# A seven-product mm2: ScalarE copies the first product's PSUM bank in two halves, each behind its row block, with mm1's last activation behind both

## The chip, the cores and the metric

The kernel runs on one core of a Trainium2 chip. The metric is device time in microseconds (us) of one execution. TensorE is called PE, and its weight loads PEld; VectorE is DVE, ScalarE is ACT, GpSimd is POOL, SyncE is SP. Each engine works off its own queue in order, and engines wait for one another through semaphores. Matrix products are accumulated in PSUM, which has eight banks of 128 partitions x 512 f32; the other memory is SBUF.

## The reference: chunk attention, then a two-layer MLP

```python
# q, k, v: 8 batches, 8 heads, 576 rows, 64 columns, f32; chunks of 64 rows
scores = scale * q_chunk @ k_chunk.T            # 64 x 64 within a chunk
attn = softmax(scores)
x = (attn @ v_chunk) -> [4608 tokens, 512]      # the heads side by side
h = gelu_exact(x @ w_in)                        # 512 -> 2048
out = h @ w_out                                 # 2048 -> 512
```

Attention is small. Most of the work is the two matrix products of the MLP: mm1, with the gelu behind it, and mm2.

## The kernel before

**Tiles.** The tokens are cut into nine tiles of 512. Tiles 0 to 7 hold the first eight chunks of one batch each; tile 8 holds the ninth chunks of all eight batches. The loop over t (at the end of the kernel) runs `phase(t, ...)`, which is mm1 and then mm2 of tile t. The attention of tile t + 1 is put into mm2 of tile t by small functions in the dictionary `e2`: the functions under key i are run where mm2 says `also(i)`. Weights and activations are bf16, sums are f32. The order of every engine's work is the order in which the program issues it; no scheduler changes it. The tile framework adds the semaphore waits, by the tiles that instructions read and write.

**Seven products.** From tile 3 on (`FIRST7 = 3`), mm2 multiplies in the manner of Strassen and Winograd: the hidden layer h of a tile is cut into 2 x 2 blocks (token half, half of the hidden rows), w_out likewise, and seven products of blocks take the place of eight. The price is sums of blocks of h (`h_s`) and of w_out (`w_t`), and sums of products that have to be copied from bank to bank.

**mm1 (`mm1_groups`).** It is issued by a string of words, `FOUR` for tiles 3 to 8. `3d` is product 3 of group d (L676, four matmuls of 128 columns of weights by 256 tokens); `c1d`, `c2d`, `c3d` copy a bank (L713 on ACT, L724 on ACT or DVE); `a1d`, `a2d` add on DVE (L727); `g21d` is the gelu of row block 2, token half 1, of group d (L683, on ACT): it reads an SBUF sum and writes blocks 14 and 15 of h for the first token half. `h1`, `h2`, `h3` are sums of blocks of h on DVE (L575, L576). The string ends with `... g12d g21d h2 h3`. The sums h2 and h3 read what g11d, g12d and g22d write, and not what g21d writes.

**mm2 (`mm2_seven`).** It takes PSUM banks X, Y and Z from a pool of three, each a tile of two row blocks by 256 columns (2 x 256 f32, one bank). The steps at its start:

- first product into X (L780, matmuls at L745): row block m = 0, eight matmuls of 128x256, then row block m = 1, eight more. `product` calls its argument `behind(m)` after each row block; here that does nothing
- ACT copies the whole of X to Y (L781), so that the next product can be added to it in Y while X goes on with another
- `also(1)`: for tiles 3 to 6 the table load for Exp on ACT (L962), and for tiles 3 to 7 `rows_av`, the 64 small attention products on PE (L346), the last of them into Z, and `rows_x` on DVE
- the second product, into Y, on top of the copy (L754, with the block sum `h_s` from h1, h2 and h3); ACT copies Y out as s2 (L787)
- the third product, into X on top of the first (L788), which reads the blocks of h that g21d writes; ACT copies X out (L789)
- the other four products, and the block sums h_third (L580) and h_fourth (L584) on DVE; h_fourth too reads what g21d writes

Tile 8 goes through `last_seven` instead. There the first product is copied by ACT to SBUF (L815), other products follow into other banks, and the row blocks of the last two products have banks of their own (`Zs`).

Of the kernel before, what the change touches and what calls it, by code (L numbers as in the profile page):

```python
# [11 lines left out]
def kernel(  # L12
# [317 lines left out]
    def by_halves(t):  # L330
        return tiles[t]["x"][:].rearrange("p g m -> p (g m)").rearrange("p (s g e) -> p s g e", s=2, g=G)
# [183 lines left out]
    DV, AC, PO = nc.vector.tensor_copy, nc.scalar.copy, nc.gpsimd.tensor_copy  # L515
# [70 lines left out]
    def in_blocks():  # L586
        return w_in_sb[:].rearrange("p (c k) (r q f e) -> p c k r q f e", c=2, r=2, q=2, e=P)
# [26 lines left out]
    def x_sums(t, which=(1, 3, 2, 4)):  # L614
# [7 lines left out]
        for i in which:  # L622
# [14 lines left out]

    FOUR = """begin 1a 1b c1a 1c 6a 7a c1b c2a 6b 5a 2a c1c 6c c2b 5b 7b c3a g11a a1a c3b c2c 3a a1b 1d 4a g22a 4b
               g12a c1d 2b a2a g22b 6d 5c g21a a2b 2d 7c h1 g11b c3c c2d 2c g11d 5d a1c 7d c3d 3c g21b 4c g11c 3b a1d
               g22c 4d g12c g12b 3d a2c a2d g21c g22d g12d g21d h2 h3"""  # L640

    FOURS = range(FIRST7, NT)
    PROGRAMS = {1: LATE, 2: THIRD, **{t: FOUR for t in FOURS}}

    def mm1_groups(t, extra, between={}):
# [3 lines left out]
        h = st["h"][:].rearrange("p f (m e) -> p f m e", m=2)  # L649
        b11, b12, b21, b22 = x_blocks(t)  # L650
        w = in_blocks()
        TT, add = nc.vector.tensor_tensor, mybir.AluOpType.add
        banks, sums = {}, {}
        four = t in FOURS
        tags = {"a": ("y_1", "y_2"), "b": ("y_5", "rc" if four else "y_2"), "d": ("y_1", "rc")}
# [23 lines left out]
        def gelu(g, r, m):  # L679
# [2 lines left out]
                   (1, 0): lambda: sums[g, 0], (1, 1): lambda: sums[g, 1]}[r, m]()  # L682
            nc.scalar.activation(h[:, j:j + 2, m], src[:], Act.Gelu)  # L683

        for word in PROGRAMS.get(t, PROGRAM).split():
            for u in extra.pop(word, ()):
                u()
            if word == "start":
                begun = mm1_slot(t, [plain.pop(0) for _ in range(4)], between, 1)
            elif word == "sums":  # L690
                x_sums(t)
            elif word == "p" and t == 1:
                begun.pop()()
            elif word == "p":
                f = plain.pop(0)
                bank = ps_tp.tile([P, MT], f32, tag="tp", name="h_ps")
                for ks in range(KS):
                    nc.tensor.matmul(bank[:].rearrange("p (s e) -> p s e", s=2), w_in_sb[:, ks, f * P:(f + 1) * P],  # L698
                                     by_halves(t)[:, :, ks] if t >= FIRSTX else
                                     st["x"][:, ks, :].rearrange("p (s e) -> p s e", s=2),  # L700
                                     start=(ks == 0), stop=(ks == KS - 1))
                nc.scalar.activation(st["h"][:, f, :], bank[:], Act.Gelu)
            elif word in hs:
                if t >= FIRST7:
                    h_sums(t, *hs[word])
            elif word[0].isdigit():
                prod(word[1], int(word[0]))
            elif word[0] == "g":
                gelu(word[3], int(word[1]) - 1, int(word[2]) - 1)
            elif word[:2] == "c1":  # L710
                g = word[2]
                banks[g + "Y"] = ps_mm.tile([P, 2, TH], f32, tag="mm", name="h_Y")
                AC(banks[g + "Y"][:], banks[g + "X"][:])  # L713
            elif word[:2] in ("c2", "c3"):
                g, i = word[2], int(word[1]) - 2
                if g != "c":
                    tag = tags[g][i]
                    sums[g, i] = work.tile([P, 2, TH], f32, tag=tag, name=f"h_{g}", bufs=2 if tag == "rc" else 1)
                elif i == 0:
                    pool, tag = (hsum, "s3") if t < B else (ypool, "y")  # L720
                    pair = pool.tile([P, 4, TH], f32, tag=tag, name="h_sb")
                    sums[g, 0] = pair[:, 0:2]
                    sums[g, 1] = pair[:, 2:4]
                (AC if i == 0 else DV)(sums[g, i][:], banks[g + "Y"][:])  # L724
            elif word[0] == "a":
                g, i = word[2], 2 - int(word[1])
                TT(sums[g, i][:], banks[g + "Z"][:], sums[g, i][:], op=add)  # L727
# [13 lines left out]
    def product(out, lhs, rhs, fresh, behind=lambda m: None, ms=range(TH // P)):  # L741

        for m in ms:
            for f in range(FH):
                nc.tensor.matmul(out[m], lhs[:, f, m * P:(m + 1) * P], rhs[:, f, :],  # L745
                                 start=fresh and f == 0 and (m == 0 or len(out) == 3), stop=(f == FH - 1),
                                 skip_group_check=True)
            behind(m)
# [8 lines left out]
    def halves(bank):  # L757
        return [bank[:, 0], bank[:, 1]]

    def mm2_seven(t, at={}):  # L760

        def also(i):
            for u in at.get(i, ()):
                u()
        st = tiles[t]
        h = st["h"][:].rearrange("p (k f) (m e) -> p k f m e", k=2, m=2)
        w = w_out_sb[:].rearrange("p (k f) (n e) -> p k f n e", k=2, n=2)
        T = [None] + [w_t[i] for i in range(1, 5)]
        def bank_mm():
            return ps_mm.tile([P, 2, NH], f32, tag="mm", name="y_ps")  # L770
        X, Y = bank_mm(), bank_mm()
        s2, s5 = (work.tile([P, 2, NH], f32, tag=nm, name=nm, bufs=1) for nm in ("y_2", "y_5"))
        y = [ypool.tile([P, 2, d_model], f32, tag="y", name="y_sb") for _ in range(2)]
        TT, add = nc.vector.tensor_tensor, mybir.AluOpType.add
        if t == B:
            s1 = work.tile([P, 2, NH], f32, tag="y_1", name="y_1", bufs=1)
            last_seven(t, h, w, T, (X, Y, bank_mm()), (s1, s2, s5), y)
            return
        also(0)
        product(halves(X), h[:, 0, :, 0], w[:, 0, :, 0], True)  # L780
        AC(Y[:], X[:])  # L781
        Z = bank_mm()
        st["Z"] = Z[:].rearrange("p m n -> p (m n)")
        also(1)
        h_third(t)
        product_by_f(halves(Y), h_sum(t, 2), T[2])
        AC(s2[:], Y[:])  # L787
        product(halves(X), h[:, 1, :, 0], w[:, 1, :, 0], False)  # L788
        AC(y[0][:, :, :NH], X[:])  # L789
        store(t, 0, 0, y)  # L790
        product(halves(Y), h_sum(t, 1), T[1], False)
        AC(s5[:], Y[:])
        h_fourth(t)
        also(2)
        product(halves(Z), h[:, 1, :, 1], T[4], True, lambda m: also((2, m)))
        TT(s2[:], Z[:], s2[:], op=add)
        also(3)
        W = bank_mm()
        product(halves(W), h_sum(t, 3), T[3], True)
        TT(y[1][:, :, NH:], W[:], s5[:], op=add)  # L800
        TT(y[1][:, :, :NH], W[:], s2[:], op=add)
        store_whole(t, 1, y)
        also(4)
        product(halves(Y), h_sum(t, 4), w[:, 1, :, 1], False)
        AC(y[0][:, :, NH:], Y[:])
        store(t, 0, 1, y)
        also(5)

    def last_seven(t, h, w, T, banks, sums, y):

        (X, Y, Z), (s1, s2, s5) = banks, sums
        TT, add = nc.vector.tensor_tensor, mybir.AluOpType.add
        Zs = [Z[:, 0], ps_at.tile([P, NH], f32, tag="at", name="y_ps")[:], None]
        product(halves(X), h[:, 0, :, 0], w[:, 0, :, 0], True)
        AC(s1[:], X[:])  # L815
        V = ps_at.tile([P, 2, NH], f32, tag="at", name="y_ps")
        product(halves(V), h[:, 1, :, 0], w[:, 1, :, 0], True, ms=(0,))
        product(halves(Y), h_sum(t, 2), T[2], True)
        h_fourth(t)
        TT(s2[:], Y[:], s1[:], op=add)  # L820
        product(halves(V), h[:, 1, :, 0], w[:, 1, :, 0], False, ms=(1,))
        h_third(t)
        TT(y[0][:, :, :NH], V[:], s1[:], op=add)
        product(halves(Y), h_sum(t, 1), T[1], False)
        TT(s5[:], Y[:], s1[:], op=add)
        W = ps_mm.tile([P, 2, NH], f32, tag="mm", name="y_ps")
        product(halves(W), h_sum(t, 4), w[:, 1, :, 1], True)
        TT(y[0][:, :, NH:], W[:], s5[:], op=add)
        store_rows(0, slice(0, 2), y)

        def row_block(m, nh):
            cols = slice(nh * NH, (nh + 1) * NH)
            TT(y[1][:, m, cols], Zs[m], (s2, s5)[nh][:, m], op=add)
            if nh == 0:
                store_rows(1, slice(m, m + 1), y, cols)
            elif m == 1:
                store_rows(1, slice(0, 2), y, cols)
        product(Zs, h_sum(t, 3), T[3], True, lambda m: row_block(m, 1))
        product(Zs, h[:, 1, :, 1], T[4], False, lambda m: row_block(m, 0))
# [358 lines left out]
```

## Time and profile before

| what | value |
|---|---|
| runs | median 269.9 us of 3 (269.69 to 271.59) |
| the profiled execution | 270.21 us, its span 268.3 us |
| granted TensorE clock, mean | 0.996 of full speed |
| PE busy | 261.1 us, 97% of the span |
| DVE, ACT, POOL busy | 204.0, 187.0, 78.6 us |
| mm2 of tiles 3 to 7 begins at | 120.49, 146.86, 173.12, 199.78, 226.11 us |
| mm2 of tile 8 begins at | 251.60 us |

The span runs from the first to the last instruction. A row of the timeline gives the start in the span, the time taken, the engine, the line of the kernel, the operation with the tiles that it writes and reads, and a count of equal neighbours (x16); square brackets say how long the engine had been idle before it and what ended that. A row of groups gives, behind a bar, total busy time and the mean ns of one; in the list of waits the three numbers are the total, the number and the longest wait, in us. In a row of a stretch the columns are its bounds, its length, the busy time of PE, PEld, DVE, ACT and POOL, the granted clock, the DMA share and GB/s. The end of a matmul is modelled: it includes the way through the array, and matmuls overlap, so a group of 16 takes less than 16 times one.

### The profile page before, as it was taken

To read this page: it belongs to the slowest core of one execution; us is meant where nothing else is said; L and a number is where in the kernel's file an instruction comes from. 1 tells how busy PE (TensorE), PEld (TensorE's weight loads), DVE (VectorE), ACT (ScalarE), POOL (GpSimd) and SP (SyncE) were. 2 spreads that over 40 slices of the span, in tenths; PEclk is the share of its full clock that TensorE was granted. 3 is DMA by queue.
4 is the path that set the end of the run, shared out by engine and by line. 5 is a ranking of instruction groups with operands and counts; after the bars stand their busy time and mean duration, and the time that the engine had idled before them with its cause. 6 is when DMAs were issued, how large, how long until landed. Compare 5 with 4: busy or idle time off the path is not lost.

```text
span 268.3 us, 7560 instructions
## 1 busy us (share of the span) xinstructions
PE 261.1 (97%) x3092; PEld 195.7 (73%) x3092; DVE 204.0 (76%) x372; ACT 187.0 (70%) x364; POOL 78.6 (29%) x127
## 2 busy tenths in 40 slices
PE   7999999999999999999999999999999999999993
PEld 3564454486448654888888888888888888888882
DVE  2574776979898879689669956995799769957872
ACT  3467756897767967897689669957895799329800
POOL 2735667360471062323026003603053030000000
PEclk9999999999999999999999999999999999999998
DMA  6999999998979979988999999998787770330005
GB/s 222 269 352 404 396 397 252 240 257 201 334 200 230 272 192 217 279 184 135 202 273 256 193 208 231 279 199 215 231 195 153 161 203 2 72 134 33 1 4 156
DMA packets 127075, 56.59 MB, mean 211 GB/s; under 512 B 103488, under 2 KB 120896, under 8 KB 127040
## 3 DMA queue, kind: packets, MB, share of 16 engines
q1 hardware_dynamic: 126592, 55.59, 81.4%
q10 hardware_dynamic: 448, 0.52, 0.7%
q8 instruction: 24, 0.39, 0.6%
q14 instruction: 11, 0.09, 0.1%
HBM read 36.70 MB, written 9.44 MB: 172 GB/s over the span
## 4 chain that ended last, share of the span: by engine, by line
PE 92%; DVE 2%; ACT 2%; DMA 1%; issue 1%; POOL 0%; SPq 0%; ACTq 0%; DVEq 0%; POOLq 0%
PE y_ps L745 24%; PE h_Y L676 15%; PE y_ps L865 12%; PE h_Z L676 10%; PE h_X L676 9%; PE h_ps L537 6%; PE y_ps L890 4%; PE y_ps L754 4%; PE s_ps L246 2%; PE h_ps L698 1%; DMA arrival<-in_k_dram 1%; PE tp L170 1%; ACT y_ps L781 1%; PE h_ps L551 1%; PE warm L957 1%; PE rc_ps L483 1%
## 5 line engine op out<-in xcount | busy, mean ns | idle before, releaser
L676 PEld LDWEIGHTS <-w_in_s 128*128 128x128 bf16 x480 | 46.8, 98 | 6.5 <-DVE x_t L624 0.5
L676 PEld LDWEIGHTS <-w_in_sb 128*128 128x128 bf16 x360 | 35.1, 98 | 6.5
L676 PE MATMUL h_X<-x,w_in_sb 128*128 128x256 bf16 x240 | 33.7, 273 | 0.0
L164 POOL CAST q_nat<-arrival 128x512 bf16<-128x512 f32 x33 | 19.4, 626 | 47.5 <-DMA arrival<-in_k_dram 33.0
L865 PE MATMUL y_ps<-w_out_sb,h 128*128 128x512 bf16 x144 | 33.0, 380 | 0.0
L676 PE MATMUL h_Y<-x_t,w_in_s 128*128 128x256 bf16 x240 | 32.7, 272 | 0.2 <-DVE x_t L624 0.2
L745 PEld LDWEIGHTS <-h_s 128*128 128x128 bf16 x304 | 29.7, 98 | 3.6 <-issue 0.2
L745 PEld LDWEIGHTS <-h 128*128 128x128 bf16 x288 | 27.9, 98 | 3.3
L217 POOL CAST v_nat<-arrival 128x1024 bf16<-128x1024 f32 x14 | 16.7, 1202 | 43.4 <-DMA arrival<-in_v_dram 43.3
L164 POOL CAST k_nat<-arrival 128x512 bf16<-128x512 f32 x34 | 22.8, 706 | 19.1 <-DMA arrival<-in_k_dram 15.1
L745 PE MATMUL y_ps<-w_t,h_s 128*128 128x256 bf16 x208 | 24.8, 273 | 0.0
L865 PEld LDWEIGHTS <-h 128*128 128x128 bf16 x144 | 13.4, 98 | 15.0 <-issue 0.2
L745 PE MATMUL y_ps<-w_out_sb,h 128*128 128x256 bf16 x192 | 22.9, 273 | 0.0
L962 ACT ACT_TABLE_LOAD x16 | 20.5, 1283 | 1.0 <-PEq L1182 0.7
L683 ACT ACTIVATE h<-h_Y 128x512 bf16<-128x512 f32 x30 | 17.7, 594 | 2.5 <-PE h_Y L676 1.9
L713 ACT COPY h_Y<-h_X 128x512 f32<-128x512 f32 x30 | 17.0, 582 | 2.8 <-PE h_X L676 2.6
L683 ACT ACTIVATE h<-h_X 128x512 bf16<-128x512 f32 x30 | 17.8, 596 | 1.3 <-PE h_X L676 0.6
L676 PE MATMUL h_Z<-x_t,w_in_s 128*128 128x256 bf16 x120 | 18.0, 273 | 0.0
L676 PE MATMUL h_Y<-x,w_in_s 128*128 128x256 bf16 x120 | 17.7, 273 | 0.0
L676 PE MATMUL h_Z<-x_t,w_in_sb 128*128 128x256 bf16 x120 | 17.4, 272 | 0.0
L253 ACT ACTIVATE pT<-s_ps 128x512 bf16<-128x512 f32 x28 | 14.5, 601 | 2.3 <-PE s_ps L246 2.3
L724 DVE COPY h_a<-h_Y 128x512 f32<-128x512 f32 x8 | 5.5, 692 | 13.1 <-PE h_Y L676 13.1
(145 smaller groups left out, 491.4 us busy)
## 6 DMA issues: line engine op xcount, KB each, us to landing
arrival<-in_q_dram SPq DMA_DIRECT2D x7, 1024.0 KB
arrival<-in_k_dram SPq DMA_DIRECT2D x24, 256.0 KB
out_dram<-y_sb SPq DMA_DIRECT2D x23, 256.0 KB
arrival<-in_v_dram SPq DMA_DIRECT2D x20, 256.0 KB
arrival<-in_moe_w_out_dram SPq DMA_DIRECT2D x4, 1024.0 KB
arrival<-in_v_dram SPq DMA_DIRECT2D x30, 128.0 KB
out_dram<-y_sb SPq DMA_DIRECT2D x5, 512.0 KB
arrival<-in_moe_w_in_dram SPq DMA_DIRECT2D x4, 512.0 KB
```

The source lines that it names most:

```text
L164: copy(st[nm][:, g].rearrange("p j r d -> p r j d"), st[nm + "f"][:, 2 * g:2 * g + 2])
L217: copy(st["v"][:, part[0], part[1], :D], st["vf"][:, part[0], part[1]])
L253: nc.scalar.activation(pT[:].rearrange("p u (c j) -> p u c j", j=J), s_ps[g2][c][:].rearrange("p u (j c) -> p u c j", j=J), Act.Exp, scale ...
L537: nc.tensor.matmul(h_ps[a][:], w_in_sb[:, ks, f * P:(f + 1) * P], st["x"][:, ks, :], start=(ks == 0), stop=(ks == KS - 1))
L676: nc.tensor.matmul(banks[g + name][:, i], lhs[:, kk, i], rhs[:, kk], start=fresh and i == kk == 0, stop=(kk == 1), skip_group_check=True)
L683: nc.scalar.activation(h[:, j:j + 2, m], src[:], Act.Gelu)
L713: AC(banks[g + "Y"][:], banks[g + "X"][:])
L745: nc.tensor.matmul(out[m], lhs[:, f, m * P:(m + 1) * P], rhs[:, f, :], start=fresh and f == 0 and (m == 0 or len(out) == 3), stop=(f == FH ...
L754: nc.tensor.matmul(out[m], lhs[:, f, m * P:(m + 1) * P], rhs[:, f, :], start=False, stop=(f == FH - 1), skip_group_check=True)
L865: nc.tensor.matmul(y_ps[:], st["h"][:, f, ms * P:(ms + 1) * P], w_out_sb[:, f, :], start=(f == 0), stop=(f == FF - 1))
L890: nc.tensor.matmul(tiles[t]["y_ps", ms][:], tiles[t]["h"][:, f, ms * P:(ms + 1) * P], w_out_sb[:, f, :], start=(f == 0), stop=False)
L962: nc.scalar.activation(act_scratch[:], rest[:, 0:1], func)
```

## The change

Three edits. The word `g21d` leaves the string `FOUR`; the same activation is kept as a function, `gelu_last[t]`. In `mm2_seven` the copy of X to Y is given to `product` as `behind(m)`: ScalarE copies row block 0 when row block 0 is done, and row block 1 when row block 1 is done, 128x256 each, and the kept activation follows behind both. In `last_seven` (tile 8) the kept activation is issued behind the first product and ahead of the copy to SBUF. The lines behind the edits move down by 1 to 4: the matmuls of L745 are L748 in the changed kernel, L754 is L757, L781 is L783, L787 is L790.

```diff
@@ FOUR
-               g22c 4d g12c g12b 3d a2c a2d g21c g22d g12d g21d h2 h3"""
+               g22c 4d g12c g12b 3d a2c a2d g21c g22d g12d h2 h3"""
+    gelu_last = {}
@@ mm1_groups
+        if four:
+            gelu_last[t] = lambda: gelu("d", 1, 0)
@@ mm2_seven
-        product(halves(X), h[:, 0, :, 0], w[:, 0, :, 0], True)
-        AC(Y[:], X[:])
+        product(halves(X), h[:, 0, :, 0], w[:, 0, :, 0], True, lambda m: AC(Y[:, m], X[:, m]))
+        gelu_last[t]()
@@ last_seven
         product(halves(X), h[:, 0, :, 0], w[:, 0, :, 0], True)
+        gelu_last[t]()
         AC(s1[:], X[:])
```

## Prediction

> **What bounds the kernel now.** I began with the page: the busy times, the slices, and the chain that ended last.
>
> ```profile
> span 268.3 us, 7560 instructions
> PE 261.1 (97%) x3092; PEld 195.7 (73%) x3092; DVE 204.0 (76%) x372; ACT 187.0 (70%) x364; POOL 78.6 (29%) x127
> PEclk9999999999999999999999999999999999999998
> PE 92%; DVE 2%; ACT 2%; DMA 1%; issue 1%; POOL 0%; SPq 0%; ACTq 0%; DVEq 0%; POOLq 0%
> ```
>
> TensorE holds 92% of the chain and is busy 97% of the span. A busy PE could still hide waits, so next comes the list of what PE waited for, whole:
>
> ```profile
> PE warm L957 <- DVE ones_c L59: 1.2, 1, 1.2
> PE tp L170 <- POOL k_nat L164: 0.6, 1, 0.6
> PE av_ps L497 <- issue: 0.3, 1, 0.3
> PE h_Y L676 <- DVE x_t L624: 0.2, 1, 0.2
> PE sum_ps L443 <- ACT pT L436: 0.2, 1, 0.2
> ```
>
> Only one of these (0.2 us, L676) lies in the seven-product stages. PE runs there without a pause: whatever makes PE pause is added to the time, and there is next to nothing to win by removing a wait. The place of the change is the start of each seven-product mm2, in tiles 3 to 7. The timeline of tile 3, where the first product begins at 120.49:
>
> ```profile
> 120.24 0.62 ACT L683 ACTIVATE h<-h_sb 128x512 bf16<-128x512 f32 x1
> 120.39 1.74 PEld L745 LDWEIGHTS <-h 128*128 128x128 bf16 x16
> 120.49 1.91 PE L745 MATMUL y_ps<-w_out_sb,h 128*128 128x256 bf16 x16
> 120.77 0.62 ACT L683 ACTIVATE h<-h_d 128x512 bf16<-128x512 f32 x1
> 121.28 0.58 ACT L683 ACTIVATE h<-h_Y 128x512 bf16<-128x512 f32 x1
> 121.76 0.63 ACT L683 ACTIVATE h<-h_d 128x512 bf16<-128x512 f32 x1
> 122.33 0.63 PEld L346 LDWEIGHTS <-pT 64*64 64x64 bf16 x64 [0.21 <-issue]
> 122.49 0.57 ACT L781 COPY y_ps<-y_ps 128x512 f32<-128x512 f32 x1
> 123.00 1.74 PEld L754 LDWEIGHTS <-h_s 128*128 128x128 bf16 x16
> 123.08 1.28 ACT L962 ACT_TABLE_LOAD   x1
> 123.12 1.91 PE L754 MATMUL y_ps<-w_t,h_s 128*128 128x256 bf16 x16
> 123.39 0.43 DVE L576 TENSOR_TENSOR h_s<-h_s,h 128x512 bf16<-128x512 bf16 x1
> 124.38 0.20 ACT L962 ACTIVATE act_scratch<-rest 128x1 f32<-128x1 bf16 x1
> 125.11 0.58 ACT L787 COPY y<-y_ps 128x512 f32<-128x512 f32 x1 [0.54 <-PE y_ps L754]
> ```
>
> The 16 matmuls of the first product start 0.109 us apart: 16 weight loads take 1.74, the last of them 0.098. Beside them ScalarE works off four activations. The last two are g12d (121.28) and g21d (121.76), the one that is moved. The copy L781 runs from 122.49 to 123.06, while PE does 64 small attention products (weight loads from 122.33 to 122.96). The next product's weights load at 123.00, 0.04 later, and its first matmul is at 123.12, 0.12 behind its weights; the first product's followed its weights by 0.10. So L781 holds PE up by 0.02 at most. The chain goes through L781 all the same, but it only ties with the attention products.
>
> **The change part by part.**
>
> *The gelu g21d moves from ahead of the copy to behind it.* It has the same shape and length on the same queue. What it writes (blocks 14 and 15 of h, first token half) is read by the second product into X and by h_fourth, not by h2, h3 or the next product. ScalarE's queue behind it: the table load and its scratch activation (tiles 3 to 6), then the copy s2 (L787). Nothing is priced here as long as s2 starts on time; this is checked at the end of the sum.
>
> *The copy is split and its first half issued behind row block 0.* Both halves of X lie in one PSUM bank, as one tile. The two kernels' built instruction orders, put side by side with their semaphore waits, show what this does: in tiles 3 to 7 the ninth matmul of the first product, the first of row block 1, gets a wait for ScalarE that it did not have, with the count that the first half copy reaches. So row block 1 does not run beside the half copy; it stands behind it. Queued behind the waiting matmul is all of PE: seven more matmuls, the attention products, and the rest of mm2. The other differences are harmless: the attention products that write Z's bank wait for PE's own past work instead of ScalarE's, one weight load in the second product into X waits for the moved gelu, and s2 loses a wait. DVE, POOL and SP issue the same instructions in the same order, all DMAs included. Tile 8's order is the same on every engine: there the gelu is only named at another place of the program.
>
> Why there must be a wait can be seen in the last tile, which does read one row block while PE computes the next:
>
> ```profile
> 262.22 1.91 PE L745 MATMUL y_ps<-w_t,h 128*128 128x256 bf16 x16
> 263.29 0.42 DVE L833 TENSOR_TENSOR y_sb<-y_ps,y 128x256 f32<-128x256 f32 x1 [0.45 <-PE y_ps L745]
> ```
>
> PE runs through its 16 matmuls without a break while VectorE reads block 0 at 263.29, but there the code gives the two row blocks separate banks (Zs). X has one. The Trainium skill, PSUM — Partial Sum Buffer, section "PSUM bank collisions raise a hardware error", says that a TensorE write and a ScalarE read of one bank in the same partitions must be kept apart by semaphores even where their columns differ. By that rule the wait cannot be had away with this layout, and the sum is the one below; without it the sum of the change would be nothing. No run shown here tries the overlap.
>
> *Price of the wait.* It is worked out from the start of the first product, in tile 3. Block 0's last matmul starts at 7 x 0.109 = 0.76 and ends about 0.27 later, at 1.03 (16 matmuls: the last starts at 1.64 and the group ends at 1.91). ScalarE answered 0.09 after the group's end (122.40 to 122.49), so PE would allow the half copy at 1.12. ScalarE is not free then: g12d starts at 0.79, and the next instruction in its queue started 0.48 later, at 1.27. The half copy takes that place. The trace has no 128x256 copy of ScalarE; the nearest rows:
>
> ```profile
> L781 ACT COPY y_ps<-y_ps 128x512 f32<-128x512 f32 x5 | 2.9, 570 | 0.5
> L436 ACT ACTIVATE pT<-s_ps 128x256 bf16<-128x256 f32 x8 | 2.6, 383 | 1.8 <-PE s_ps L432 1.8
> L389 ACT ACTIVATE pT<-s_ps 128x512 bf16<-128x512 f32 x4 | 2.2, 594 | 2.0 <-PE s_ps L385 2.0
> L411 ACT COPY rb<-r 32x16 f32<-32x16 f32 x16 | 3.2, 202 | 1.0 <-DVE r L405 0.8
> ```
>
> Halving the columns of an exp saves 594 - 383 = 211 ns, so I take 570 - 211 = 359 ns, 0.36; the ends are 0.20 (a copy of 16 columns) and 0.57 (no saving at all). PE answered the full copy within 0.06 (123.06 to 123.12). The ninth matmul then starts at 1.27 + 0.36 + 0.06 = 1.69 instead of 8 x 0.109 = 0.87: a stall of 0.82 us.
>
> *Is any of it given back?* From there the row keeps its pace: eight matmuls, the attention products, the next product, each 0.82 later. The second half copy waits for block 1's end: the last matmul starts at 1.69 + 0.76 = 2.45, ends at 2.72, copy from 2.81 to 3.17. The next product, 2.63 after the start before, is now due at 3.45: the copy is covered by 0.28, but it was covered before too, so the shorter tail returns at most the 0.02 above. g21d then starts near 3.1 and ends near 3.75; the table load (1.28) and scratch (0.20) end near 5.25. The product that s2 waits for ends at 3.45 + 1.91 = 5.36. So s2 is still released by PE; its idle time of 0.54 shrinks to about 0.2. Were that cover gone, a late s2 would meet PE only after the whole next product (1.74). The sums h2 and h3 keep their times on DVE while PE comes later, which cures one small wait, in tile 6:
>
> ```profile
> 199.78 1.91 PE L745 MATMUL y_ps<-w_out_sb,h 128*128 128x256 bf16 x16
> 200.58 0.59 ACT L683 ACTIVATE h<-h_Y 128x512 bf16<-128x512 f32 x1
> 201.06 0.63 ACT L683 ACTIVATE h<-h_d 128x512 bf16<-128x512 f32 x1
> 202.40 1.97 PE L754 MATMUL y_ps<-w_t,h_s 128*128 128x256 bf16 x16
> 203.76 0.33 PEld L754 LDWEIGHTS <-h_s 128*128 128x128 bf16 x4 [0.17 <-DVE h_s L576]
> ```
>
> There the product took 1.97 instead of 1.91: 0.06 back. The same rows show that tile 6 has tile 3's spacing (g12d 0.80 after the product's start, next activation 0.48 later), and so does the last tile concerned, 7:
>
> ```profile
> 226.11 1.91 PE L745 MATMUL y_ps<-w_out_sb,h 128*128 128x256 bf16 x16
> 226.91 0.59 ACT L683 ACTIVATE h<-h_Y 128x512 bf16<-128x512 f32 x1
> 227.38 0.63 ACT L683 ACTIVATE h<-h_d 128x512 bf16<-128x512 f32 x1
> ```
>
> *The sum.* 5 x 0.82 = 4.10, less 0.06: +4.0 us. The profiled execution took 270.21 (span 268.3 and 1.9 around it), 0.3 above the median 269.9 of the runs shown; it becomes 274.2, and the median 273.9. Bounds of one stall: 1.27 + 0.20 + 0.06 - 0.87 = 0.66 with the shortest copy; 1.37 + 0.57 + 0.06 - 0.87 = 1.13 if the half copy is no shorter and starts only when g12d has ended (0.79 + 0.58). Five of them: 3.3 to 5.65 us.
>
> **The rivals.**
>
> *Faster, by a shorter copy tail.* The chain passes L781 in five tiles, and its part behind the product's end shrinks from 0.57 to 0.36. If that were PE's wait, five times 0.21, 1.05 us, would come back: 268.8. It needs two things: the next product bound by the copy and not by the attention products (the tie above leaves 0.02 a tile, 0.1 in all), and a row block 1 that is not held. Against the second stands the added wait. It decides only from the point where the stall is under 0.21 a tile, and the lower bound is 0.66.
>
> *No change.* The wait is there but is met when PE arrives. Row block 1 is due at 0.87, and the half copy would have to be over by 0.81, when block 0 itself ends at 1.03. So it can't be met in time; only slack of PE elsewhere could swallow 4 us, and PE's waits from 120 us on come to 0.2. Time 269.9.
>
> *Much slower: the stalls cost clock.* After PE's last matmul (262.22 + 1.91 = 264.13) the span has 4.2 us without matmuls, and the granted clock of the last stretch is the only one that is low:
>
> ```profile
> 0.00:8.00 8.00, 6.25 (x24) 2.71 (x25) 1.75 (x5) 2.07 (x3) 2.79 (x15) 1.00 0.73 241
> 251.60:268.30 16.70, 12.53 (x114) 10.86 (x111) 9.24 (x15) 2.49 (x5) 0.00 (x0) 0.94 0.24 65
> ```
>
> It lost 0.06 x 16.70 = 1.0 us of clock. If each of five stalls lost as much, the time would be 273.9 + 5.0 = 278.9. Against it: the 0.6 us wait of the transposes (L170) lies in the first stretch, whose clock is 1.00, and 0.82 is near 0.6 and far from 4.2. The Trainium skill, TensorE: Matmul & The Clock Gate, bears on it from both sides: its section "Why this matters for your kernels" asks only that PE never idles over about 3 us, by which nothing is lost here; its section "A second HAM failure mode: psum-queue depth-cycling" tells of short idles between groups of matmuls that did throttle the clock, by which this rival holds. The row of the first stretch agrees with the former.
>
> **How the numbers follow.** About 1% of the time, 2.7 us, is what a measurement of this kernel tells from no change; five stalls of 0.54 make that, under the lower bound of 0.66. Chances: the stalls as summed 0.90; stalls with lost clock 0.03; no change 0.06; faster by the shorter tail 0.01, and that by under 1%, so faster by over 1% has 0.01 at most. Slower 0.93, same 0.06, faster 0.01. The forecast is 273.9. The range goes from 3.3 above the lowest run (269.69, so 273.0) to 5.65 above the median (275.6); the clock rival and no change, 0.09 together, stay outside.
>
> **What would show it.** In the changed profile PE's first product (L748) splits into two groups of 8, with about 0.8 us between them, ended by ScalarE's copy (L783), in tiles 3 to 7. L783 counts 10 copies of 128x256 near 360 ns, the first of each pair starting about 1.27 after the product. The next product (L757) starts about 3.45 after it, where 2.63 stood. s2 (now L790) is still released by PE. Tile 8 is unchanged. I am wrong if the 16 matmuls still run in 1.91 us, if the half copy comes much later than 1.4, or if the granted clock drops in slices before the last.

## The result and the profile after

The changed kernel is slower: median 274.43 us (273.65 to 275.51, 6 runs) against 270.44 (269.69 to 271.59, 6 runs), ratio 1.0124 with a 95% interval of 1.0089 to 1.0160. The forecast was 273.9 us, in a range of 273.0 to 275.6, from a median of 269.9; three more runs of the kernel before have moved that median up by 0.5. The page of the changed kernel, the same rows as before:

```profile
span 271.6 us, 7550 instructions
PE 259.2 (95%) x3077; PEld 194.7 (72%) x3092; DVE 204.7 (75%) x372; ACT 187.7 (69%) x369; POOL 77.2 (28%) x127
PEclk9999999999999999999999999999999999999998
PE 86%; ACT 4%; SPq 4%; DMA 2%; issue 1%; DVE 1%; POOL 0%
```

The span grew by 3.3 us while every engine's busy time stayed within 2 us (15 of PE's matmul records are missing in this trace, 3077 of 3092, which lowers its figure). So the time is idle time of PE. What PE waited for from 120 us on, the whole list:

```profile
PE y_ps L748 <- ACT y_ps L783: 3.3, 5, 0.7
PE h_Z L677 <- DVE h_d L730: 0.4, 1, 0.4
```

Five waits of the first product for the half copy, one in each of tiles 3 to 7, where there was none. The timeline of tile 3:

```profile
119.80 0.97 PEld L748 LDWEIGHTS <-h 128*128 128x128 bf16 x9
119.91 1.04 PE L748 MATMUL y_ps<-w_out_sb,h 128*128 128x256 bf16 x8
120.71 0.59 ACT L684 ACTIVATE h<-h_Y 128x512 bf16<-128x512 f32 x1
121.18 0.39 ACT L783 COPY y_ps<-y_ps 128x256 f32<-128x256 f32 x1
121.62 1.03 PE L748 MATMUL y_ps<-w_out_sb,h 128*128 128x256 bf16 x8 [0.68 <-ACT y_ps L783]
122.75 0.36 ACT L783 COPY y_ps<-y_ps 128x256 f32<-128x256 f32 x1 [1.18 <-PE y_ps L748]
123.02 0.63 ACT L684 ACTIVATE h<-h_d 128x512 bf16<-128x512 f32 x1
123.25 1.64 PEld L757 LDWEIGHTS <-h_s 128*128 128x128 bf16 x16
123.25 1.92 PE L757 MATMUL y_ps<-w_t,h_s 128*128 128x256 bf16 x16
124.90 1.74 PEld L748 LDWEIGHTS <-h 128*128 128x128 bf16 x16
125.21 0.59 ACT L790 COPY y<-y_ps 128x512 f32<-128x512 f32 x1
```

The 16 matmuls have become two groups of 8. The second begins 1.71 us after the first (119.91 to 121.62) and not 0.87: a stall of 0.84. (The 0.68 in brackets is counted from the modelled end of the eighth matmul.) Nine weight loads stand ahead of it: the weights of the ninth matmul are in place, it is the matmul that waits. The third product's weights come 5.10 after those of the first (119.80 to 124.90), where 4.36 stood before: 0.74 are lost in this tile.

### The profile page after: what moved, and what is told of

Read it like the earlier page. It is cut to its first block, busy times and chain, and to the rows that moved or that the text cites. A ratio compares the mean times of both kernels' runs of the same rounds, so it can differ in the third digit from the quotient of the medians.

```text
span 271.6 us, 7550 instructions
## 1 busy us (share of the span) xinstructions
PE 259.2 (95%) x3077; PEld 194.7 (72%) x3092; DVE 204.7 (75%) x372; ACT 187.7 (69%) x369; POOL 77.2 (28%) x127
## 4 chain that ended last, share of the span: by engine, by line
PE 86%; ACT 4%; SPq 4%; DMA 2%; issue 1%; DVE 1%; POOL 0%
PE y_ps L748 23%; PE h_Y L677 14%; PE y_ps L869 11%; PE h_X L677 10%; PE h_Z L677 9%; PE h_ps L537 5%; PE y_ps L894 4%; PE y_ps L757 3%; ACT h L684 3%; DMA arrival<-in_moe_w_in_dram 2%; SPq L149 2%; PE s_ps L246 2%; SPq L108 1%; PE h_ps L701 1%; PE av_ps L346 1%
## 5 line engine op out<-in xcount | busy, mean ns | idle before, releaser
L748 PEld LDWEIGHTS <-h 128*128 128x128 bf16 x288 | 27.8, 98 | 7.4 <-issue 4.2
L869 PE MATMUL y_ps<-w_out_sb,h 128*128 128x512 bf16 x137 | 31.7, 379 | 0.9 <-issue 0.8
L748 PEld LDWEIGHTS <-h_s 128*128 128x128 bf16 x304 | 29.8, 98 | 3.6 <-issue 0.2
L217 POOL CAST v_nat<-arrival 128x1024 bf16<-128x1024 f32 x14 | 15.5, 1112 | 48.6 <-DMA arrival<-in_v_dram 48.5
L748 PE MATMUL y_ps<-w_out_sb,h 128*128 128x256 bf16 x192 | 23.7, 272 | 3.3 <-ACT y_ps L783 3.3
L164 POOL CAST k_nat<-arrival 128x512 bf16<-128x512 f32 x34 | 21.8, 675 | 16.7 <-DMA arrival<-in_k_dram 13.2
L748 PE MATMUL y_ps<-w_t,h_s 128*128 128x256 bf16 x208 | 24.8, 272 | 0.0
```

The lines of the kernel that those rows point to most:

```text
L164: copy(st[nm][:, g].rearrange("p j r d -> p r j d"), st[nm + "f"][:, 2 * g:2 * g + 2])
L217: copy(st["v"][:, part[0], part[1], :D], st["vf"][:, part[0], part[1]])
L869: nc.tensor.matmul(y_ps[:], st["h"][:, f, ms * P:(ms + 1) * P], w_out_sb[:, f, :], start=(f == 0), stop=(f == FF - 1))
```

## The experiments

Two theories went into them. **A**: row block 1 is held because the half copy reads the PSUM bank that PE is to write next, and it starts only when ScalarE's queue comes to it. **B**, the rival: the cost is ScalarE's own, one more copy and the activation moved behind it. In the edits below, minus is the changed kernel. The distance from the first product's weights to the third's is the measure within a tile. The table gives it for tile 3, and its change against the kernel before added up over tiles 3 to 7 of the traces. Times come from the ratio to the kernel before on the same chip.

| kernel | first to third product in tile 3, us | change in the five tiles, us | ratio, 95% interval |
|---|---|---|---|
| before | 4.36 | | |
| changed | 5.10 | +3.5 | 1.0124 (1.0089 to 1.0160) |
| both half copies late | 4.54 | +0.8 | 1.0048 (1.0020 to 1.0075) |
| whole copy, gelu behind | 4.36 | -0.1 | 1.0009 (0.9981 to 1.0036) |
| split, gelu ahead | 5.62 | +6.1 | 1.0255 (1.0214 to 1.0295) |
| first half copy reads elsewhere | 4.27 | -0.5 | 1.0009 (0.9978 to 1.0041) |
| no copy | 4.27 | -0.4 | 0.9988 (0.9963 to 1.0013) |
| half copy ahead of g12d | 4.92 | +2.7 | 1.0091 (1.0060 to 1.0123) |
| row block 1 in a bank of its own | 4.42 | +0.2 | 1.0019 (0.9986 to 1.0051) |

### Both half copies late

```diff
-        product(halves(X), h[:, 0, :, 0], w[:, 0, :, 0], True, lambda m: AC(Y[:, m], X[:, m]))
+        product(halves(X), h[:, 0, :, 0], w[:, 0, :, 0], True)
+        for m in range(2):
+            AC(Y[:, m], X[:, m])
         gelu_last[t]()
```

> As the changed kernel, but both half copies are issued behind both row blocks; the gelu still follows them. Theory A (row block 1 is held because the half copy reads the bank that it writes): nothing holds the ninth matmul any more, PE's 16 matmuls run in 1.91 us again. The second half copy waits for the first one's end, so the pair ends near 2.00 + 0.36 + 0.06 + 0.36 = 2.78 us after the product's start instead of 2.57, and the next product starts 0.2 later than in the kernel before: five times 0.2, 271.4 us against 270.4 before and 274.4 changed. Theory B (the cost is ScalarE's: one more copy and the gelu behind it, whatever PE does at row block 1): the copies and their number are the same, so 274.4.

Ratio 1.0048, 1.3 us more than before; expected were 1.0 by A and 4.0 by B. The timeline of tile 3:

```profile
122.01 1.74 PEld L748 LDWEIGHTS <-h 128*128 128x128 bf16 x16
122.12 1.91 PE L748 MATMUL y_ps<-w_out_sb,h 128*128 128x256 bf16 x16
124.12 0.75 ACT L785 COPY y_ps<-y_ps 128x256 f32<-128x256 f32 x2 [0.62 <-PE y_ps L748]
124.92 1.91 PE L757 MATMUL y_ps<-w_t,h_s 128*128 128x256 bf16 x16 [0.22 <-ACT y_ps L785]
126.55 1.74 PEld L748 LDWEIGHTS <-h 128*128 128x128 bf16 x16
```

The first product runs through again. Two half copies, one after the other, take 0.75 where the whole copy took 0.57. PE now waits 0.22 for them ahead of the second product, and the third comes 0.18 later than before, which is the difference of the two. B falls: with the same copies and the same moved gelu most of the loss is gone.

### The moved gelu alone

```diff
-        product(halves(X), h[:, 0, :, 0], w[:, 0, :, 0], True, lambda m: AC(Y[:, m], X[:, m]))
+        product(halves(X), h[:, 0, :, 0], w[:, 0, :, 0], True)
+        AC(Y[:], X[:])
         gelu_last[t]()
```

> Only the moved gelu: one whole copy of X behind both row blocks, and g21d behind it. Theory A: the copy starts when PE ends (2.00 us after the product's start), as before, since ScalarE was free by 1.90 even with the gelu ahead; no change, 270.4 within 0.5. Theory B: the gelu behind the copy delays the table load and s2, 272 to 274.

Ratio 1.0009, no difference. From the timeline of tile 3:

```profile
121.33 1.91 PE L748 MATMUL y_ps<-w_out_sb,h 128*128 128x256 bf16 x16
123.33 0.57 ACT L784 COPY y_ps<-y_ps 128x512 f32<-128x512 f32 x1 [0.62 <-PE y_ps L748]
123.95 1.91 PE L757 MATMUL y_ps<-w_t,h_s 128*128 128x256 bf16 x16
```

With the gelu out of its way ScalarE stands idle for 0.62 us, and the copy still starts 2.00 us after the product, when PE is done with it. The gelu had covered time in which ScalarE had nothing else to do.

### The split alone, with the gelu ahead

```diff
+        gelu_last[t]()
         product(halves(X), h[:, 0, :, 0], w[:, 0, :, 0], True, lambda m: AC(Y[:, m], X[:, m]))
-        gelu_last[t]()
```

> Only the split: the half copies stand behind their row blocks as in the changed kernel, and the gelu goes back ahead of them. Theory A: the first half copy takes its place one activation later (0.48 us), so row block 1 starts near 2.2 us after the product's start instead of 1.71; five times 0.48 on top of 274.4, 276.8 us. Theory B (the moved gelu is the cost): back to about 270.4 to 271.5.

Ratio 1.0255, 6.9 us more than before, where A asked for 6.4 (276.8 against 270.4). The half copy's place in ScalarE's queue sets the stall:

```profile
121.42 1.04 PE L748 MATMUL y_ps<-w_out_sb,h 128*128 128x256 bf16 x8
122.69 0.63 ACT L684 ACTIVATE h<-h_d 128x512 bf16<-128x512 f32 x1
123.21 0.38 ACT L784 COPY y_ps<-y_ps 128x256 f32<-128x256 f32 x1
123.64 1.03 PE L748 MATMUL y_ps<-w_out_sb,h 128*128 128x256 bf16 x8 [1.18 <-ACT y_ps L784]
```

One activation more ahead of the copy moves it from 1.27 to 1.79 after the product's start, and row block 1 from 1.71 to 2.22. That is 0.51 a tile, against 0.48 expected. The five tiles make 6.1 us by the table; the 0.8 left of 6.9 lies within the interval (0.0041 of 271.3 is 1.1 us), and in this trace PE also waits 1.1 us in mm1 for sums on VectorE, against 0.2 before.

### The first half copy reads elsewhere

```diff
-        product(halves(X), h[:, 0, :, 0], w[:, 0, :, 0], True, lambda m: AC(Y[:, m], X[:, m]))
+        product(halves(X), h[:, 0, :, 0], w[:, 0, :, 0], True,
+                lambda m: AC(Y[:, m], X[:, m] if m else rest[:, :NH]))
         gelu_last[t]()
```

> As the changed kernel, with one operand exchanged: the first half copy reads a constant tile of zeros in SBUF instead of row block 0 of X, so row block 0 of the first product is left out of the second sum. ScalarE issues the same instructions of the same sizes in the same order, and reads X only when row block 1 is done. Theory A: the ninth matmul is not held, the first product runs in 1.91 us; the shorter tail of the copy returns up to 0.1 a tile, 269.9 to 270.4 us. Theory B: 274.4, as in the changed kernel.

Ratio 1.0009 (0.9978 to 1.0041): the loss is gone, and a gain of 0.5 us can be neither seen nor excluded. In the trace:

```profile
121.19 1.91 PE L748 MATMUL y_ps<-w_out_sb,h 128*128 128x256 bf16 x16
122.47 0.39 ACT L784 CAST y_ps<-rest 128x256 f32<-128x256 bf16 x1
123.20 0.36 ACT L784 COPY y_ps<-y_ps 128x256 f32<-128x256 f32 x1 [0.34 <-PE y_ps L748]
123.70 1.92 PE L757 MATMUL y_ps<-w_t,h_s 128*128 128x256 bf16 x16
```

The profile calls this half copy a CAST, since the zeros are bf16; it takes the same 0.39 at the same distance (1.28) as in the changed kernel, and PE does not pause. It is the reading of X, and nothing else about the half copy, that holds PE.

### No copy at all

```diff
-        product(halves(X), h[:, 0, :, 0], w[:, 0, :, 0], True, lambda m: AC(Y[:, m], X[:, m]))
+        product(halves(X), h[:, 0, :, 0], w[:, 0, :, 0], True)
         gelu_last[t]()
...
-                nc.tensor.matmul(out[m], lhs[:, f, m * P:(m + 1) * P], rhs[:, f, :], start=False, stop=(f == FH - 1),
+                nc.tensor.matmul(out[m], lhs[:, f, m * P:(m + 1) * P], rhs[:, f, :], start=f == m == 0, stop=(f == FH - 1),
```

> What the whole copy costs PE in the kernel before: no copy of X to Y at all, the gelu g21d issued behind the first product, and the second product starts a fresh sum in Y (the first product is left out of it). If the copy only ties with the attention products, as the prediction put it (0.02 us a tile), 270.3 us and the next product still starts 2.6 us after the first. If it holds PE up by the 0.1 us a tile that the changed kernel's trace suggests (its next product follows the attention products 0.11 closer), the next product starts 2.5 after the first one and the time is 269.9.

Ratio 0.9988 (0.9963 to 1.0013), too near to tell in the time; the trace tells it:

```profile
121.93 1.91 PE L748 MATMUL y_ps<-w_out_sb,h 128*128 128x256 bf16 x16
124.44 1.64 PEld L757 LDWEIGHTS <-h_s 128*128 128x128 bf16 x16
124.44 1.92 PE L757 MATMUL y_ps<-w_t,h_s 128*128 128x256 bf16 x16
```

The second product starts 2.51 after the first; in the kernel before it was 2.63 (120.49 to 123.12). So the whole copy did hold PE up there, by 0.12, and by 0.09 at the third product. That is also all that any treatment of this copy could win: about 0.5 us, 0.2%, less than these runs can resolve.

### The half copy ahead of g12d

```diff
-            gelu_last[t] = lambda: gelu("d", 1, 0)
+            gelu_last[t] = [lambda: gelu("d", 0, 1), lambda: gelu("d", 1, 0)]
...
-        product(halves(X), h[:, 0, :, 0], w[:, 0, :, 0], True, lambda m: AC(Y[:, m], X[:, m]))
-        gelu_last[t]()
+        product(halves(X), h[:, 0, :, 0], w[:, 0, :, 0], True, lambda m: (AC(Y[:, m], X[:, m]), gelu_last[t][m]()))
+        h_sums(t, 6, 8)
```

The words g12d and h3 leave the string `FOUR`; tile 8 issues both activations and h3 behind its first product.

> As the changed kernel, but the first half copy goes ahead of g12d, and g12d (with the sum h3 that needs it) behind that half copy. Theory A with ScalarE's queue setting the start: the half copy now starts when row block 0 has ended, at 1.12 us after the product's start instead of 1.27, row block 1 at 1.55 instead of 1.71: 0.15 a tile, 273.6 us against 274.4 of the changed kernel. If the half copy's start is not set by the queue but by PE's row block 0 and the wait itself, it still starts at 1.27 and the time stays 274.4.

Ratio 1.0091 (1.0060 to 1.0123), 2.5 us. The first half copy now waits for PE, and PE for it:

```profile
120.23 1.04 PE L748 MATMUL y_ps<-w_out_sb,h 128*128 128x256 bf16 x8
121.36 0.36 ACT L783 COPY y_ps<-y_ps 128x256 f32<-128x256 f32 x1 [0.23 <-PE y_ps L748]
121.77 1.03 PE L748 MATMUL y_ps<-w_out_sb,h 128*128 128x256 bf16 x8 [0.50 <-ACT y_ps L783]
```

It starts at 1.13, row block 1 at 1.54 (expected 1.12 and 1.55). With nothing of ScalarE's queue left in it the stall is still 0.67: the way from PE to the copy, the copy, and the way back. That this is better than the changed kernel is seen in the trace alone; the two intervals of the ratio overlap (to 1.0123 here, from 1.0089 there).

### Row block 1 in a bank of its own

```diff
-        product(halves(X), h[:, 0, :, 0], w[:, 0, :, 0], True, lambda m: AC(Y[:, m], X[:, m]))
+        W1 = ps_at.tile([P, 2, NH], f32, tag="at", name="y_w1")
+        blocks = [X[:, 0], W1[:, 0]]
+        product(blocks, h[:, 0, :, 0], w[:, 0, :, 0], True, lambda m: AC(Y[:, m], blocks[m]), apart=True)
         gelu_last[t]()
```

With `apart`, row block 1 starts its own sum; in `rows_av` the attention's three banks of this pool are taken in turn, so that the one that W1 had comes last.

> As the changed kernel, with a bank of its own for row block 1 of the first product: block 0 goes to X, block 1 to a bank W1 of the attention's pool, and the half copies go from X and from W1 to the two halves of Y, each behind its row block. The third sum, which goes on in X, lacks row block 1 of the first product. The attention product that takes W1's place in the pool is put last but two, and may wait a little for the second half copy. Theory A, with the shared bank as the reason for the wait: row block 1 runs beside the first half copy, the ninth matmul is 0.87 us behind the first, the next product starts 2.5 to 2.6 us after the first instead of 3.3, and the time is that of the kernel before or up to 0.5 less, 269.9 to 270.5 us against 274.4 changed. If the half copy delays row block 1 for another reason than the bank (the order in which the copies are issued, ScalarE's load), the ninth matmul stays at 1.7 and the time at 274.

Ratio 1.0019 (0.9986 to 1.0051), the time of the kernel before:

```profile
122.07 1.04 PE L749 MATMUL y_ps<-w_out_sb,h 128*128 128x256 bf16 x8
122.94 1.04 PE L749 MATMUL y_w<-w_out_sb,h 128*128 128x256 bf16 x8
123.35 0.38 ACT L786 COPY y_ps<-y_ps 128x256 f32<-128x256 f32 x1
124.07 0.36 ACT L786 COPY y_ps<-y_w 128x256 f32<-128x256 f32 x1 [0.34 <-PE y_w L749]
124.73 1.92 PE L758 MATMUL y_ps<-w_t,h_s 128*128 128x256 bf16 x16
```

Row block 1 follows 0.87 behind row block 0, and the first half copy runs beside it (from 123.35). The second product comes 2.66 after the first, later than expected (2.5 to 2.6): one attention product waits for the bank that the second half copy gives free. The order of issue and the copies are those of the changed kernel, and what differs for row block 1 is where it is written. So what the wait is for is shown: that both row blocks share X. W1 is another bank and also another tile, and this run does not tell the two apart. That parts of one tile need not wait for each other as such can be seen in SBUF, where h is one tile: in the changed kernel's tile 3 the first product reads blocks of h from 119.91 on, and ScalarE writes other blocks of h at 120.71. No run tests it in PSUM.

## Why the prediction was right, point by point

**The wait and its place** were right. The ninth matmul waits for the first half copy in all five tiles, tile 8 has no such wait, and the runs above exclude the number of copies, ScalarE's load and the gelu's place as the reason for it.

**The stall's terms** held: the half copy started at 1.27 (forecast 1.27), took 0.39 (0.36) and let row block 1 go at 1.71 (1.69). Over all ten half copies, from the list for their line:

```profile
L783 ACT COPY y_ps<-y_ps x10: 357/365/386, 121.2 to 231.5; 128x256 f32<-128x256 f32 x10
```

The five that PE waits for, the first of each pair, took 373 to 386 ns and the five second ones 357, near the 359 that were taken from halving an exp; the end of the first one in tile 3, at 121.57, was answered by PE 0.05 later. The 0.15 us that ScalarE's queue added was shown by the run with the half copy ahead of g12d.

**The term that was mis-sized** is the tie: "So L781 holds PE up by 0.02 at most." It held PE up by about 0.10. I read the 0.12 between the second product's first weight load and its matmul as pace, because the first product had 0.10. But the first product follows matmuls that start about 0.11 apart, and its weights are loaded one matmul ahead. The second follows the attention products, 64 weight loads in 0.63; there, without a wait, the two records stand at one time (124.44 and 124.44 in the run with no copy). The 0.12 was a wait for the copy, with the weights already loaded. So the shorter tail of the split copy gave back 0.10 a tile, and the loss a tile is 0.84 - 0.10 = 0.74, not 0.82.

**That the time met the forecast so closely is luck.** In the profiled execution tiles 3 to 7 lost 0.74, 0.69, 0.69, 0.68 and 0.74, which is 3.5 us where 4.0 were forecast. (In tiles 4 and 5 the half copy started at 1.24 and not 1.27; in tile 6 the small wait of 0.06 went away, as forecast.) The medians differ by 4.0, in an interval of 2.4 to 4.3 us (0.0089 and 0.0160 of 270.4) that holds 3.5 as well; the runs of each kernel spread over 1.9. In the same execution the way from mm2 of tile 3 to mm2 of tile 8 grew by 3.85 (first weights at 119.80 and 254.75, against 120.39 and 251.49), and 0.36 of that is another wait, in mm1 of tile 4. It comes from a sum on VectorE that took 1.15 us beside a cast on GpSimd; VectorE then ran without a pause up to the sum that PE waited for:

```profile
142.37 2.37 POOL L217 CAST v_nat<-arrival 128x1024 bf16<-128x1024 f32 x2
142.68 1.15 DVE L576 TENSOR_TENSOR h_s<-h_s,h 128x512 bf16<-128x512 bf16 x1
146.67 0.60 PE L677 MATMUL h_Z<-x_t,w_in_sb 128*128 128x256 bf16 x4 [0.36 <-DVE h_d L730]
```

In the kernel before the same sum fell between two casts (142.47, where the next cast came at 143.08):

```profile
142.47 0.42 DVE L576 TENSOR_TENSOR h_s<-h_s,h 128x512 bf16<-128x512 bf16 x1
143.08 2.29 POOL L164 CAST k_nat<-arrival 128x512 bf16<-128x512 f32 x4 [1.87 <-issue]
```

The casts wait for loads, and they fall at other places in each of the traces. Whether the change makes such meetings more frequent is open: waits of this kind also stand in the traces of runs without the stall (0.3 us in the run that reads elsewhere).

**s2** had less slack than forecast. About 0.2 us were to be left; ScalarE was free at 125.16 (the scratch activation 124.96 + 0.20) and s2 started at 125.21, 0.04 after the second product's end (123.25 + 1.92), so nearly nothing was left. PE had come 0.10 earlier than forecast, by the tie: the second product started 3.34 after the first, and not 3.45. No PE wait followed.

**The rivals.** The faster case failed where the prediction put it, since row block 1 is held; but its other condition, a second product bound by the copy, was nearer to being met than the 0.02 said. The clock rival failed. What the prediction counted as 1.0 us of lost clock was no lost time: in the kernel before the granted clock was 1.00 from 251.60 to the last matmul's end at 264.13, and 0.77 in the 4.20 us behind it, where PE has nothing left to do. The granted clock is at 9 tenths or more in every slice but the last, as before, and even the run with stalls of 1.18 has a mean clock of 0.998. The Trainium skill, TensorE: Matmul & The Clock Gate, section "Why this matters for your kernels", which asks that gaps between bursts of matmuls stay under about 3 us, agrees with these traces; the short-idle throttling of its section "A second HAM failure mode: psum-queue depth-cycling" did not show at five stalls of 0.5 to 1.2 us, some 27 us apart.

**What stays open.** Whether the chip itself would bear the overlap in one bank was not tried, since the wait cannot be taken away without a race. The Trainium skill, PSUM — Partial Sum Buffer, section "PSUM bank collisions raise a hardware error", says that it would not: a write of TensorE and a read of ScalarE that meet in one bank and the same partitions raise an error, at other columns too. No run here shows it. Nor does a run try two tiles in one bank, or one tile in two.

## What to carry to other kernels

In these runs the writer and the reader of a split copy out of PSUM overlapped only where the parts lay in different banks, as tiles of their own; two halves of one bank turned a copy that was nearly hidden behind other work into a stall of the writer, in tile 3 0.84 us for a copy of 0.39. Before splitting, ask what the engine does during the copy now: here 64 attention products covered all but 0.1 us, so the split had 0.1 us a tile to win. And look at which activation stands ahead of the copy in its queue: one more of them cost another 0.5 us a tile.

## What the runs showed of the hardware that was not expected

A matmul record 0.12 us behind its weight load can be a wait: weights are loaded ahead while the matmul is held (nine loads ahead of the eight matmuls, then 0.68 of waiting). Only what ran before tells it from pace: the third product of the kernel before stands 0.11 behind its weights (124.75 and 124.86) and waits for nothing. Two half copies in a row took 0.75 us against 0.57 for the whole copy: half the columns cost two thirds of the time. And the same bf16 sum on VectorE took 0.42 or 1.15 us, the longer beside a cast on GpSimd. In the traces before and after, the 128x512 sums of L575 and L576 that meet no cast all took 0.41 to 0.43 us, and the nine that meet one 0.55 to 1.15. The Trainium skill, SBUF — State Buffer, section "Who interferes with whom", says that a VectorE instruction with two inputs in SBUF contends with a GpSimd instruction that reads SBUF. The rows agree; no run moves the casts away to test it.
